# Retention with two tokens to a partition and 64x64 products throughout

## The chip, the cores and the metric

The kernel runs on one core of a Trainium2 chip. TensorE (PE) multiplies; VectorE (DVE) and ScalarE (ACT) do elementwise work and read what TensorE left in PSUM; GpSimd (POOL) here mainly issues DMAs that load and change type; SyncE (SP) issues stores and DMA transposes. Each engine works through its own list in order and waits at semaphores. The metric is the device time in microseconds of one launch. Three runs of the kernel before gave a median of 290.66 us (290.3 to 291.85).

## The reference

Retention over 8 batches, 8 heads, 576 tokens and 64 features a head, then a two-layer product with a hard-swish between:

```python
scores = scale * np.matmul(q, k.transpose(0, 1, 3, 2))          # scale = 1/8
gamma = 1.0 - 2.0 ** (-5.0 - np.arange(H, dtype=np.float32))
Dmat = np.where(rel >= 0, gamma[:, None, None] ** rel[None, :, :], 0.0)   # rel = query - key
ret = np.matmul(scores * Dmat[None, :, :, :], v)
x = ret.transpose(0, 2, 1, 3).reshape(B * S, H * D)             # 4608 x 512
h = x @ w_in                                                    # 512 x 2048
out = (h * np.clip(h + 3.0, 0.0, 6.0) / 6.0) @ w_out            # 2048 x 512
```

## The kernel before

Retention is computed in chunks. A piece is 128 tokens of one batch, with all 8 heads; a batch has four of them, and its last 64 tokens share a piece with those of the next batch ("rest" pieces). There are 36 pieces, and four make a block of 512 tokens, so there are nine blocks. For each piece:

- k and q are brought into a form with the features on the partitions. For pieces 0 to 7 TensorE does it: `k_by_pe` (L318) transposes 128x128 blocks against an identity, `q_by_pe` (L331) multiplies by scaled diagonals in 64x64 products, and ScalarE copies the results out of PSUM. From piece 8 on, SP issues DMA transposes: `transpose_k` (L340) and `transpose_q` (L346), the latter after VectorE has scaled q and v together by powers of gamma (L345).
- `scores` (L356) multiplies k by q for each head, contracting over 64 features; the result is masked by VectorE (L365, L637), half of it by way of a ScalarE copy (`raw`; L767, L633) and a second mask operation (L770).
- `inter` (L282) multiplies q by the running state of the batch, and `intra` (L290) multiplies v by the masked scores; both accumulate in PSUM. The casts at L265 turn them into `xt`, the input of the first matrix product.
- `update_mm` (L384) multiplies k by v, contracting over 128 tokens, and `update_state` (L398 to L402) adds this to the state and decays it.

The first matrix product (`g1`, L411, and L434 for parts of its columns) makes 16 chunks of 128 x 512, each passed through ScalarE (L418) and VectorE (L419). The second is done plainly for block 0 (`g2`, L461), and for blocks 1 to 8 with seven products on half-sized operands (`product`, L520; the sums on VectorE at L494, the results gathered at L530 to L544).

The order of work is written out by hand; there is no planner. The start handles pieces 0 to 3, with filler products on zeros (`warm`, L215) where TensorE would wait. During block 0's second product, steps are put in behind its 16 units, for pieces 4 to 7. `seven_block(kb, mine, next_)` then runs for kb = 1 to 7: between the seven products of block kb it takes the scores of block kb+1's second pair, masks them, does all output products of block kb+1 (`all_outputs`), its state updates and the scores of the first pair of the block after that; then follows the first product of block kb+1. `last_block` does the seven products of block 8, whose rows are the rest tokens, and stores each result as it comes (`store_rest`, L451), on SP and, for the last ones, on ACT's queue too. `store2` (L592) stores the other blocks, `store` (L444) block 0.

Four PSUM banks carry the tag `ph` and are shared by everything; `sc` has two banks, `tu` and `o` one each.

Of the kernel before, what the change touches and what calls it, by code (L numbers as in the profile page):

```python
# [13 lines left out]
ALU = mybir.AluOpType  # L14
# [3 lines left out]
def kernel(  # L18
# [74 lines left out]
    EARLY = 4  # L93
    BY_PE = 8
    SEVEN = 1
    NBUF = 6
    KBUF = 8

    def by_twos(b, s0):

        return q[b, :, s0:s0 + P, :].rearrange("h (g t) d -> g h (t d)", t=2)

    def q2_tile(c):

        tag, bufs = (("part1", 1), ("part5", 1), ("part6", 1), ("osb2", 3))[c % EARLY]
        return work.tile([HALF, H, 2 * D], FP16, tag=tag, bufs=bufs, name=f"q2_{c}")

    def load(c, parts="kqv"):
        if c not in loaded:
            kn = nat.tile([P, H, D], FP16, tag="kn", bufs=KBUF, name=f"kn_{c}")  # L110
            qv = nat.tile([P, 2, H, D], FP16, tag="qv", bufs=NBUF, name=f"qv_{c}")
            loaded[c] = {"kn": kn, "qv": qv}
            if c < BY_PE:
                loaded[c]["q2"] = q2_tile(c)
        to = {"k": (loaded[c]["kn"], k), "q": (loaded[c]["qv"][:, 0], q),
              "v": (loaded[c]["qv"][:, 1], v)}
        for dst, src in (to[part] for part in parts):
            for p0, b, s0, n in pieces[c][3]:
                if src is q and c < BY_PE:
                    nc.gpsimd.dma_start(loaded[c]["q2"], by_twos(b, s0))  # L120
                    continue
                nc.gpsimd.dma_start(dst[p0:p0 + n],  # L122
                                    src[b, :, s0:s0 + n, :].rearrange("h s d -> s h d"))
# [8 lines left out]
    def load_wout(c0, c1):  # L132
# [9 lines left out]
    k0 = work.tile([P, H, D], FP32, tag="osb", bufs=4, name="whole_k_0")  # L142
    nc.sync.dma_start(k0, k[0, :, 0:P, :].rearrange("h s d -> s h d"))
    v0 = work.tile([P, H, D], FP32, tag="osb", bufs=4, name="whole_v_0")
    loaded[0] = {"kn": nat.tile([P, H, D], FP16, tag="kn", bufs=KBUF, name="kn_0"),
                 "q2": q2_tile(0), "v": v0}
    nc.gpsimd.dma_start(loaded[0]["q2"], by_twos(0, 0))
# [11 lines left out]
    two = const.tile([HALF, 2], FP32)  # L159
    e2 = const.tile([HALF, 2, H], FP32)  # L160
    for t in range(2):
        nc.vector.tensor_scalar(out=two[:, t:t + 1], in0=wide[0:HALF, HALF // 2 + 1:HALF // 2 + 2],
                                scalar1=-2.0, scalar2=float(t), op0=ALU.mult, op1=ALU.add)
        nc.vector.tensor_scalar(out=e2[:, t], in0=lnr[0:HALF], scalar1=two[:, t:t + 1],
                                scalar2=None, op0=ALU.mult)
    g2q = const.tile([HALF, 2, H], FP32)
    nc.scalar.activation(g2q, e2, ACTF.Exp)
    tl = const.tile([P, H], FP32)
    nc.vector.tensor_scalar(out=tl, in0=lnr, scalar1=wide[:, HALF + 1:HALF + 2], scalar2=None,
                            op0=ALU.mult)  # L170
    gq = const.tile([P, H], FP32)
    nc.scalar.activation(gq, tl, ACTF.Exp, scale=-1.0)
    gv = const.tile([P, H], FP32)
    nc.scalar.activation(gv, tl, ACTF.Exp, bias=cb[:, 1:2])
    mask_wide = const.tile([P, P + 1], FP16)
    nc.vector.tensor_scalar(out=mask_wide, in0=wide, scalar1=0.0, scalar2=None, op0=ALU.is_ge)
    mask01 = mask_wide[:, 1:P + 1]
    ident16 = const.tile([P, P], FP16)
    nc.vector.tensor_tensor(out=ident16, in0=mask01, in1=mask_wide[:, 0:P], op=ALU.subtract)

    nc.vector.memset(v0[:, 0, 0:1], 0.0)
    nc.sync.dma_start(v0, v[0, :, 0:P, :].rearrange("h s d -> s h d"))
    d2 = const.tile([HALF, 2 * H, HALF], FP16)
    nc.vector.tensor_tensor(
        out=d2, in0=ident16[0:HALF, None, 0:HALF].to_broadcast([HALF, 2 * H, HALF]),
        in1=g2q.rearrange("g t h -> g (t h)")[:, :, None].to_broadcast([HALF, 2 * H, HALF]),
        op=ALU.mult)
    gqv = const.tile([P, 2, H, D], FP16)
    nc.scalar.copy(gqv[:, 1], gv[:, :, None].to_broadcast([P, H, D]))
    nc.scalar.copy(loaded[0]["kn"], k0)  # L190
# [12 lines left out]
    def fill_gq():  # L203
        nc.scalar.copy(gqv[:, 0], gq[:, :, None].to_broadcast([P, H, D]))
# [15 lines left out]
    mask_rest = const.tile([P, P], FP16)  # L220

    def make_mask_rest():
        nc.vector.tensor_copy(mask_rest, mask01)
        nc.vector.memset(mask_rest[0:HALF, HALF:P], 0.0)

    mask_b = {"main": mask01[:, None, :].to_broadcast([P, H, P]),
              "rest": mask_rest[:, None, :].to_broadcast([P, H, P])}
# [5 lines left out]

    class Output:
        def __init__(self, cs, tags):

            self.cs, self.of = cs, len(tags)
            self.n = NCC // self.of
            self.banks = []
            for i, tag in enumerate(tags):  # L240
# [12 lines left out]
        def begins(self, c, h):  # L253
            return c == self.cs[0] and h % NCC < self.of
# [753 lines left out]
```

## Time and profile before

| What | us |
|---|---|
| median of three runs | 290.66 |
| the profiled execution, whole | 289.8 |
| its span | 288.0 |
| TensorE busy | 281.9 |
| VectorE busy | 236.5 |
| ScalarE busy | 163.0 |
| GpSimd busy | 110.7 |

The profile is of one execution. Busy times are those of one engine, with overlapping instructions counted once; the span is from the first instruction to the last. A row of the chain of work gives the start, the length and the engine, tile and line of a stretch that nothing else overlapped on the way back from the last instruction. A row of the groups gives the count of alike instructions, their busy time and the mean of one in ns, then the idle time in front of them and what ended it. "64*64" in a TensorE row is the part of the array that is used, rows by columns. SPq and ACTq are the times in which those engines issue DMAs.

### The profile page before, as it was taken

To read this page: it belongs to the slowest core of one execution; us is meant where nothing else is said; L and a number is where in the kernel's file an instruction comes from. 1 tells how busy PE (TensorE), PEld (TensorE's weight loads), DVE (VectorE), ACT (ScalarE), POOL (GpSimd) and SP (SyncE) were. 2 spreads that over 40 slices of the span, in tenths; PEclk is the share of its full clock that TensorE was granted. 3 is DMA by queue.
4 is the path that set the end of the run, shared out by engine and by line. 5 is a ranking of instruction groups with operands and counts; after the bars stand their busy time and mean duration, and the time that the engine had idled before them with its cause. 6 is when DMAs were issued, how large, how long until landed. Compare 5 with 4: busy or idle time off the path is not lost.

```text
span 288.0 us, 7104 instructions
## 1 busy us (share of the span) xinstructions
PE 281.9 (98%) x2900; PEld 182.7 (63%) x2900; DVE 236.5 (82%) x403; ACT 163.0 (57%) x267; POOL 110.7 (38%) x146
## 2 busy tenths in 40 slices
PE   8999999999999999999999999999999999999994
PEld 3554446648764786468646874687458745874583
DVE  4687649999989988998799879997999789928951
ACT  5668426784278517861776168715872486337721
POOL 8974569630696107520752064306880000000000
PEclk9999999999999999999999999999999999999998
DMA  9999999999999999991999199948995740021014
GB/s 130 168 189 195 192 167 210 171 132 138 106 183 189 138 85 168 193 118 38 135 198 145 38 144 187 130 57 129 200 121 56 104 127 2 0 76 73 2 36 109
DMA packets 149856, 35.85 MB, mean 124 GB/s; under 512 B 139584, under 2 KB 145728, under 8 KB 149824
## 3 DMA queue, kind: packets, MB, share of 16 engines
q0 software_dynamic: 111712, 18.10, 93.9%
q1 hardware_dynamic: 37808, 17.05, 32.3%
q8 instruction: 22, 0.36, 0.5%
q10 hardware_dynamic: 304, 0.26, 0.3%
q14 instruction: 10, 0.08, 0.1%
HBM read 36.70 MB, written 9.44 MB: 160 GB/s over the span
## 4 chain that ended last, share of the span: by engine, by line
PE 96%; DVE 2%; issue 0%; ACTq 0%; ACT 0%; DVEq 0%
PE ph L411 41%; PE b L520 19%; PE c L520 9%; PE a L520 5%; PE pout L461 5%; PE sc L356 4%; PE o L290 3%; PE warm L215 3%; PE ph L434 2%; PE o L282 1%; PE u L384 1%; DVE at L365 1%; PE trq L331 1%; PE trk L318 1%; ACTq L451 0%
## 5 line engine op out<-in xcount | busy, mean ns | idle before, releaser
L418 ACT ACTIVATE u<-ph,cb 128x512 f32<-128x512 f32 x144 | 98.5, 689 | 25.8 <-PE ph L411 23.3
L419 DVE SCALAR_TENSOR_TENSOR gt<-u,ph 128x512 f16<-128x512 f32 x144 | 95.6, 685 | 18.1 <-ACT u L418 15.9
L411 PE MATMUL ph<-xt,win 128*128 128x512 f16 x488 | 106.6, 379 | 0.0
L411 PEld LDWEIGHTS <-win 128*128 128x128 f16 x552 | 54.0, 98 | 63.2
L122 POOL DMA_DIRECT2D kn<-in_k_dram x39 | 33.4, 863 | 64.3 <-PE u L384 58.7
L520 PEld LDWEIGHTS <-s 128*128 128x128 f16 x512 | 49.8, 98 | 6.2 <-DVE s L494 0.2
L520 PEld LDWEIGHTS <-gt 128*128 128x128 f16 x384 | 35.8, 98 | 7.9 <-DVE gt L419 1.1
L122 POOL DMA_DIRECT2D qv<-in_v_dram x39 | 33.9, 876 | 2.3 <-DMA wout<-in_moe_w_out_dram 1.6
L520 PE MATMUL b<-tw,s 128*128 128x256 f16 x256 | 30.6, 273 | 0.0
L122 POOL DMA_DIRECT2D qv<-in_q_dram x32 | 27.3, 860 | 4.3 <-DMA qv<-in_v_dram 2.1
L265 ACT CAST xt<-o 128x512 f16<-128x512 f32 (+1 forms) x25 | 13.2, 584 | 26.0 <-PE o L290 25.9
L365 DVE TENSOR_TENSOR at<-sc,mask_wide 128x1024 f16<-128x1024 f32 x18 | 22.0, 1220 | 6.5 <-PE sc L356 6.5
L494 DVE TENSOR_TENSOR s<-gt 128x512 f16<-128x512 f16 (+1 forms) x37 | 22.7, 615 | 0.1
L530 ACT COPY part<-b 128x512 f32<-128x512 f32 x14 | 8.2, 586 | 25.6 <-PE b L520 25.6
L755 POOL COPY turn<-vs 128x1 f16<-128x1 f16 x7 | 2.6, 372 | 47.1 <-DVE vs L345 47.1
L345 DVE TENSOR_TENSOR vs<-qv,gqv 128x1024 f16<-128x1024 f16 x28 | 19.2, 686 | 0.4 <-DMA qv<-in_v_dram 0.3
L520 PE MATMUL b<-wout,gt 128*128 128x256 f16 x128 | 15.6, 273 | 0.0
L520 PE MATMUL b<-tw,gt 128*128 128x256 f16 x128 | 15.4, 273 | 0.0
L520 PE MATMUL a<-wout,gt 128*128 128x256 f16 x128 | 15.3, 273 | 0.0
L520 PE MATMUL c<-wout,s 128*128 128x256 f16 x128 | 15.3, 273 | 0.0
L520 PE MATMUL c<-tw,s 128*128 128x256 f16 x128 | 15.3, 273 | 0.0
L767 ACT CAST raw<-sc 128x512 f16<-128x512 f32 x28 | 15.0, 589 | 0.2 <-PE sc L356 0.2
(83 smaller groups left out, 271.1 us busy)
## 6 DMA issues: line engine op xcount, KB each, us to landing
kn<-in_k_dram POOLq DMA_DIRECT2D x31, 128.0 KB, 6.8
qv<-in_v_dram POOLq DMA_DIRECT2D x31, 128.0 KB, 7.6
out_dram<-olo SPq DMA_DIRECT2D x7, 512.0 KB, 3.9
out_dram<-ohi SPq DMA_DIRECT2D x7, 512.0 KB, 5.3
qv<-in_q_dram POOLq DMA_DIRECT2D x24, 128.0 KB, 7.3
wout<-in_moe_w_out_dram POOLq DMA_DIRECT2D x4, 512.0 KB, 12.3
q<-in_q_dram POOLq DMA_DIRECT2D x8, 128.0 KB, 6.1
win<-in_moe_w_in_dram POOLq DMA_DIRECT2D x8, 128.0 KB, 6.1
```

The costliest lines, as they stand in the source:

```text
L122: nc.gpsimd.dma_start(dst[p0:p0 + n], src[b, :, s0:s0 + n, :].rearrange("h s d -> s h d"))
L265: engine(xt_of(kb)[:, i::self.of, g0:g0 + len(self.cs) * P], self.banks[i].rearrange("x a c s -> x a (c s)"))
L345: nc.vector.tensor_tensor(out=vs, in0=loaded[c]["qv"], in1=gqv, op=ALU.mult)
L356: nc.tensor.matmul(banks[h2][t, p, :], qk[r, 1, p, t], qk[r, 0, p, :], start=True, stop=True)
L365: mask = lambda: nc.vector.tensor_tensor(out=at.rearrange("t a b s -> t (a b) s"), in0=sc.rearrange("t a b s -> t (a b) s"), in1=mask_b[pi ...
L411: nc.tensor.matmul(ph, win16[:, dmc, P * fc:P * fc + P], xt_of(kb)[:, dmc, :], start=(dmc == 0), stop=(dmc == NCC - 1))
L418: nc.scalar.activation(u, ph, ACTF.Relu, bias=cb[:, 0:1], scale=1.0 / 6.0)
L419: nc.vector.scalar_tensor_tensor(out=gts[kb][:, fc, :], in0=u, scalar=1.0, in1=ph, op0=ALU.min, op1=ALU.mult)
L461: nc.tensor.matmul(pout, gt[:, fc, P * mc:P * mc + P], wout16[:, fc, :], start=(fc == 0), stop=(fc == NFC - 1))
L494: nc.vector.tensor_tensor(out=sm[i][:, q], in0=one, in1=other, op=op)
L520: nc.tensor.matmul(my[chain][tt], left[:, k, P * tt:P * tt + P], right[:, k, :], start=(first and (tt == 0 or apart) and k == 0), stop=(k ...
L767: nc.scalar.copy(raw[:, h2], banks[h2])
```

## The change

All of q, k and v is loaded in one form. Two neighbouring tokens go to one partition: partition g of a half tile holds tokens 2g and 2g+1 of the piece, 512 bytes in a row for a head, where before a partition held one token and 256 bytes (q of pieces 0 to 7 was already loaded so). Two pieces, a pair, are stacked in one tile, the even piece on partitions 0 to 63 and the odd one on 64 to 127. Inside a piece the order of tokens is therefore even ones first, then odd ones; the outputs are stored with a row step of two, and each store becomes one DMA for each parity (in the last block also one for each batch and half).

All retention products become 64x64 in the array: 64 features or 64 token pairs to contract, 64 to put out, with the two pieces of a pair in the two halves of the rows. Products that were made once over 128 tokens are made twice, once for each parity. Before the second half of the state products stands a drain of TensorE, so that two row halves don't write into one bank together. The decay of the keys moves from v to k: for pieces from 8 on, VectorE scales k and q (`scaled`) and leaves v as it is, and the DMA transposes take 128 x 1024 of a pair at once. For pieces 0 to 7 both k and q are turned by 64x64 products (`turn`), and v is scaled in place. The written order at the start and around block 0 is new, as below; two fillers fewer stand there.

```diff
+    def load(c, parts="kqv"):
+        k2, par = divmod(c, 2)
...
+                r = par * HALF + p0 // 2
+                nc.gpsimd.dma_start(
+                    dst[r:r + n // 2],
+                    src[b, :, s0:s0 + n, :].rearrange("h (g t) d -> g h (t d)", t=2))
...
+    def inter_half(pair, turn):
+        order = [(pair[1 - turn], (0, 4), (2, 6)), (pair[turn], (1, 5), (3, 7))]
+        for i in range(2):
+            for o, *heads in order:
+                for h in heads[i]:
...
+                        nc.tensor.matmul(
+                            o.at(h, g), state[rows(h % 2), h // 2, :],
+                            turned(o.c // 2)[rows(h % 2), 1, h // 2, :, at + g.start:at + g.stop],
...
+    def intra(pair):
+        for cc in range(NCC):
+            for t in range(2):
+                for o in pair:
+                    k2, par = divmod(o.c, 2)
+                    for half in range(2):
+                        h = half * NCC + cc
+                        nc.tensor.matmul(
+                            o.at(h), loaded[k2]["v"][rows(par), h, t * D:t * D + D],
+                            st[k2]["at"][rows(par), h % 2, h // 2, t],
...
+    def transpose(k2, which):
+        scaled(k2, which)
+        nc.sync.dma_start_transpose(
+            turned(k2)[:, which].rearrange("x p t s -> x (p t) s"),
+            st[k2]["ks"][:, which].rearrange("s p t a d -> s (p t a d)"))
+    def begin(k2, tags=("ph", "ph")):
...
+        for p in range(NPAIR):
+            for t in range(2):
                 for h2 in range(2):
+                    for par in range(2):
+                        to = sc[:, h2] if p < 2 else more[h2]
...
+        for h2 in range(2):
+            nc.scalar.copy(raw[:, h2], more[h2])
...
+        def mask(i):
+            for h2 in range(2):
+                nc.vector.tensor_tensor(
+                    out=at[:, h2, 2 * i:2 * i + 2].rearrange("x p t u g -> x p (t u g)"),
+                    in0=(raw if i else sc)[:, h2].rearrange("x p t s -> x p (t s)"),
...
     def store_rest(mc, n, cols, src, queues):
-        rows = out.rearrange("(b s) n -> b s n", s=S)
-        for i, queue in enumerate(queues):
-            at = rows[2 * mc + i:2 * (mc + n - 1) + i + 1:2, MAIN:S, cols]
-            queue.dma_start(at.rearrange("t r n -> r t n"), src[i * HALF:i * HALF + HALF])
+        by_b = out.rearrange("(b s) n -> b s n", s=S)
+        quarter = HALF // 2
+        for j in range(n):
+            for t, queue in enumerate(queues):
+                for i in range(2):
+                    r = t * HALF + i * quarter
+                    queue.dma_start(by_b[2 * (mc + j) + i, MAIN + t:S:2, cols],
+                                    src[r:r + quarter, j])
...
+    turn(2, Q)
+    warm(2, MBLK)
+    output_new(0, ("tu", "o"))
+    turn(3, K)
+    warm(2, MBLK)
+    turn(3, Q)
+    warm(2, MBLK)
+    mask = begin(1)
+    mask(0)
     scale_v(1)
+    mask(1)
...
+    def outputs_two(pair, u_tags, between):
...
+        inter_half(pair, 0)
+        for p, t in steps:
+            u_mm(cs[0], p, t, True)
...
+        nc.tensor.drain()
...
+        inter_half(pair, 1)
+        intra(pair)
+        between()
+        for o in pair:
+            o.cast(nc.scalar.copy)
+    def step_four():
+        def between():
+            waiting["mask"] = begin(3)
+        outputs_two([Output(4, "ph"), Output(5, "o")], ("tu",), between)
+        waiting["mask"](0)
+        scale_v(3)
+        waiting["mask"](1)
         update_state(4)
         update_state(5)
     def step_six():
+        outputs_two([Output(6, "sc"), Output(7, "ph")], ("tu", "o"), lambda: None)
...
+    def all_outputs(mine, next_, ready):
+        pairs = [[Output(mine[0], "sc"), Output(mine[1], "ph")],
+                 [Output(mine[2], "ph"), Output(mine[3], "ph")]]
+        if not is_new(mine[0]):
+            for pair in pairs:
+                inter_half(pair, 0)
+            nc.tensor.drain()
+            for pair in pairs:
+                inter_half(pair, 1)
         engines = [nc.vector.tensor_copy] + [nc.scalar.copy] * 3
+        for pair in pairs:
+            intra(pair)
+            for o in pair:
+                o.cast(engines.pop(0))
+        update_mm(list(mine))
         if next_:
+            ready(next_[0] // 2)
+            load_until(next_[1] + GROUP)
...
+    steps = {3: [(turn_two, 4, "tu", "o")], 6: [(make_mask_rest,)], 9: [(turn_sc, 5)],
+             10: [(begin_by_pe, 2, ("tu", "o")), (turn, 6, K)], 11: [(turn, 6, Q, "tu")],
+             12: [(turn_two, 7, "o", "ph")], 13: [(step_four,)],
+             14: [(transpose, 4, K)]}
```

## The prediction

> **What bounds the kernel now.** I read the page's engine line first, then the chain of work that ended last, then the timelines of the places where the chain leaves TensorE.
>
> ```profile
> PE 281.9 (98%) x2900; PEld 182.7 (63%) x2900; DVE 236.5 (82%) x403; ACT 163.0 (57%) x267; POOL 110.7 (38%) x146
> PE 96%; DVE 2%; issue 0%; ACTq 0%; ACT 0%; DVEq 0%
> q0 software_dynamic: 111712, 18.10, 93.9%
> ```
>
> TensorE is busy nearly all the time and carries 96% of the chain. The load queue is as full (93.9%), but no DMA stands on the chain: loads are hidden. So half as many packets is worth nothing by itself, and the change can gain only by shortening TensorE's row of work, and lose wherever TensorE comes to wait. One steady stage of the chain in order of time (start, us, what), and the rest block's form of the same:
>
> ```profile
> 105.35 1.75 PE c L520 x16
> 107.10 0.57 PE o L282 x32
> 107.67 1.01 PE o L290 x32
> 108.68 0.50 PE u L384 x32
> 109.19 0.60 PE sc L356 x16
> 109.78 1.85 PE b L520 x16
> 254.24 0.64 PE o L282 x64
> ```
>
> A full-array group costs 1.75 behind its like and 1.85 behind retention; the seam is a price of about 0.1. State products (L282) are 64x64 already: 32 of 128 columns in 0.57, 17.8 ns each. In the rest block 64 of 64 columns took 0.64, 10 ns each.
>
> The chain leaves TensorE at the start, where masks bind, in the first block of seven products, and at the end:
>
> ```profile
> 14.10 1.23 DVE at L365
> 15.71 0.41 PE o L290 x8
> 16.12 0.98 PE ph L434 x8
> 18.99 12.09 PE ph L411 x56
> 54.74 10.36 PE ph L411 x48
> 76.30 1.14 DVE at L365
> ```
>
> **The change part by part.** Prices of VectorE and ScalarE operations, by groups:
>
> ```profile
> L637 DVE TENSOR_TENSOR at<-sc,mask_wide 128x512 f16<-128x512 f32 x2 | 1.4, 684 | 0.0
> L637 DVE TENSOR_TENSOR at<-raw,mask_wide 128x512 f16<-128x512 f16 x2 | 0.8, 420 | 0.0
> L345 DVE TENSOR_TENSOR vs<-qv,gqv 128x1024 f16<-128x1024 f16 x28 | 19.2, 686 | 0.4 <-DMA qv<-in_v_dram 0.3
> L305 DVE TENSOR_TENSOR vs<-qv,gqv 128x512 f16<-128x512 f16 x6 | 2.5, 411 | 0.0
> L365 DVE TENSOR_TENSOR at<-sc,mask_wide 128x1024 f16<-128x1024 f32 x18 | 22.0, 1220 | 6.5 <-PE sc L356 6.5
> L770 DVE TENSOR_TENSOR at<-raw,mask_wide 128x1024 f16<-128x1024 f16 x12 | 8.3, 692 | 0.0
> L767 ACT CAST raw<-sc 128x512 f16<-128x512 f32 x28 | 15.0, 589 | 0.2 <-PE sc L356 0.2
> ```
>
> *Loads.* Same count and bytes, half the descriptors, one more on POOL's queue (v of piece 0). Worth nothing: no wait on the chain ends on them.
>
> Prices on TensorE at the start: fillers, a transpose of k, and what a turn will be like.
>
> ```profile
> 1.19 3.59 PE warm L215 x8
> 6.86 0.75 PE warm L215 x3
> 34.53 0.22 PE trk L318 x4
> 34.76 0.37 PE trq L331 x16
> ```
>
> *Start-up, +1.2.* Pieces now go in pairs. A pair's masks and v scaling are 2x0.684 + 2x0.411 + 2x0.420 = 3.03 us on VectorE, about 2.75 with the overlap that neighbours show, and its output products need all of it. From 4.79, where the eight fillers end, four turns at 0.37 and nine fillers at about 0.27 (0.25 once the clock is up) put the first pair's scores at 9.0 to 9.45. Masks end at 12.05; two turns and five fillers (2.0) cover to 11.45, so 0.6 of idle. Output products, two turns behind ScalarE's cast and two copies (0.59 each), and the second pair's scores end at 15.2. Its masks run to 17.8, while TensorE has only 0.98 of columns (L434): 1.6 idle. Then 0.45 of outputs, 0.52 of state updates (64 at 8 ns) and 0.98 bring the L411 stream to 19.8 to 20.6, against 18.99: I take +1.2. Ends: -0.5 (first loads land sooner and move it all up) and +3 (a whole mask chain of 3.03 uncovered).
>
> *Block 0's second product, 31 to 55 us, +2.4.* Work: four k transposes become turns, 4x(0.37-0.22) = 0.6. State updates of 64 rows use one row half at a time, 4x0.25 against 0.61: +0.4. Two drains at 0.2: +0.4. Fewer shape seams: -0.3. That is +1.1. Waits: the scores of pair 2 stand one 0.87 unit behind a turn whose two copies take 1.18: 0.3. In the fourth step, pair 3's two raw copies are issued ahead of the two output casts: 4x0.59 = 2.36 after the scores, while TensorE has two units, 1.73, before it needs the casts: 0.65. In the sixth step the update bank is freed by VectorE after 2.75 of masks and three state operations of 0.42, 4.0, while TensorE arrives after 1.73+0.65+0.98+0.22 = 3.6: 0.4. Together 1.35. Ends: +0.5 (covers hold) and +4.5 (waits and drains double).
>
> *First block of seven, +0.8.* The mask row at 76.30 binds already. Per pair the masks go from 1.22+0.69 to 2.2 (+0.3), the scaling from 2x0.686 to 4x0.411 (+0.27), and two masks and one scaling lie ahead: +0.87. Ends 0 and 1.6.
>
> For the output stages: a state product's own length, VectorE's idle, and a transpose with the scores that need it.
>
> ```profile
> L282 PE MATMUL o<-qk,ts 64*64 64x128 f16 x192 | 4.1, 218 | 0.2 <-DVE at L365 0.2
> 113.26 0.69 DVE L419 SCALAR_TENSOR_TENSOR gt<-u,ph 128x512 f16<-128x512 f32 x1 [0.86 <-ACT u L418]
> 136.68 0.69 DVE L540 TENSOR_TENSOR olo<-part,c 128x512 f32<-128x512 f32 x1 [0.72 <-PE c L520]
> 133.65 1.19 SPq L346 DMA_TRANSPOSE qk<-vs x1
> 138.16 0.59 PE sc L356 x16
> ```
>
> *Seven output stages, +0.2 in all.* Without seams 32 products of 128 columns at four at once are 0.45, so state products 0.57 (one seam), output products (64) 0.89, updates 64 at 8 ns in 0.52, scores 32 in 0.45: 2.43 against 0.57+1.01+0.50+0.60 = 2.68, which is -0.25. The drain between the halves of the state products has no row here; the nearest is the seam, 0.1, and the farthest the 0.22 that one such product lasts (218 ns), so I take 0.2, with 0 and 0.5 as ends. The last two outputs are now cast only after all of their pair's products, so the second half of the next scores may wait 0.1 for a bank. So +0.05 each, -0.12 in the block without state products. Ends -1.8 and +3.5 over all.
>
> VectorE's extra 1.1 a block is hidden here: 0.3 in the 0.86 of idle at 113, 0.57 in the 0.72 at 136. With that cover gone it would cost its full 0.3 to 0.6. The q transpose of the next first pair, one DMA of 1024 columns for two of 512, is issued at about 133.9; at twice 1.19 of issue plus about 0.8 it lands by 137.1 to 137.9, before the scores at 138.16. That cover is thin.
>
> *The end, +3.3.* One store of the last block becomes four (32 rows, one token parity, one batch each): 8, 8 and 4 on SP for three 128-row results and 4 on ACT, then 2+2 for each of the two last pieces.
>
> ```profile
> L451 SPq DMA_DIRECT2D out_dram<-endc x5: 490/595/600, 281.2 to 284.7; - x5
> L451 ACTq DMA_DIRECT2D out_dram<-endc x3: 496/515/745, 282.6 to 284.7; - x3
> L444 SPq DMA_DIRECT2D out_dram<-osb x4: 332/348/360, 42.8 to 50.8; - x4
> L586 ACT COPY endc<-b 128x256 f32<-128x256 f32 x2 | 0.7, 373 | 4.9 <-PE b L520 4.9
> 281.16 4.05 SPq L451 DMA_DIRECT2D out_dram<-endc  x5
> 282.57 0.74 ACTq L451 DMA_DIRECT2D out_dram<-endc  x1
> 284.72 0.50 ACTq L451 DMA_DIRECT2D out_dram<-endc  x1
> ```
>
> From 281.16 SP has 16 issues in line; none is hidden, since TensorE is finishing. A smaller store has no row: between 0.348 and 0.595 each, and I take 0.45, below the 64-row stores. The last then starts at 281.16 + 15x0.45 = 287.9 against 284.7: +3.2. On ACT, four issues stand ahead of the copy of the next to last result, two ahead of the last one: 282.57 + 4x0.5 + 0.4 + 2x0.5 + 0.4 + 0.5 = 286.9, +2.2, so SP sets the end. Ends: 15x0.348 gives +1.7, 15x0.595 gives +5.4. Stores of the main blocks also double (issue 0.35 to 0.6 more); SP has room there.
>
> The sum: 1.2+2.4+0.8+0.2+3.3 = +7.9. The profiled execution took 289.8 (span 288.0), 0.9 below the median of 290.66: 297.7.
>
> **The rivals.** *Faster, by the seams.* The change removes some 25 places where the shape of products changes (13 in the output stages, a dozen in blocks 0 and 1), more than the text above credits with 0.1 to 0.15. If each were worth the whole 0.5, 12 us would go, outweighing 7.9, and the kernel takes 285.7; at the 0.15 of the rows 25 places are 3.8, half of it already in the sum. It decides from about 0.4 a seam. For: seams are visible. Against: 1.85 less 1.75 is 0.1. The Trainium skill, "TensorEngine Tiling (Array Packing)", Key Properties, says that changing the tiling mode drains the engine, which speaks for this rival; the trace agrees in kind, with 0.10 in a place, and so the size, not the rule, keeps the chance low.
>
> *About equal.* Issue prices under 0.2 at the end and mask chains covered at the start leave 1 to 2 us: 291.
>
> *Slower still, by transposes or VectorE.* Issue to landing of the q transposes of 512 columns:
>
> ```profile
> DMA to landing us min/median/max: 2.4/4.2/9.3
> ```
>
> My allowance for 1024 columns, 3.2 to 4.0, is below this median for 512. If they land 2 us after 137.5, behind loads and stores, TensorE waits 1.3 in six blocks: 305.5. The same follows if scaling in runs of 64 elements goes at the 0.684 of f32: 8x0.27 = 2.2 a block more, past VectorE's idle. For: landings reached 9.3. Against: half the load packets, and no wait of this kind on the chain now.
>
> *Slower, by issue.* The four groups of an output stage and its other scores grow from 128 products to 224 plus 32. Were 25 ns the least between products, 256 would take 6.4 a stage against 3.2, some 20 us in all: 318. The row at 254.24, 10 ns, excludes it. The Trainium skill, "TensorE: Matmul & The Clock Gate", on the 56 ns gap, gives such a floor of about 25 ns; the trace disagrees for quarter-array products, so it gets 0.02.
>
> **How the numbers follow.** My forecast 0.62 (own range 293.5 to 302), later transposes or VectorE 0.16, issue 0.02, faster 0.11, equal 0.09. The range goes from the equal case, 291.5, to the late transposes, 304.5; it leaves out faster, issue and the ends. 0.5% of 290.66, 1.45, is about what a measurement here can tell from no change: faster 0.11, same 0.09, slower 0.80.
>
> **What would show it.** At the start: L411's counterpart begins at 19.8 to 20.6, idle before the second output products ended by VectorE. Steady: a period near 29.5 without idle on TensorE. At the end: SP in issue without pause after the last results, 16 in line. Wrong would make it: a period under 29.2 (seams), idle before the first scores of a stage ended by a DMA (transposes), or SP issues under 0.3 each.

## The result, and the profile after

| | us |
|---|---|
| before, median of 4 runs beside the kernel after | 291.25 (290.3 to 294.3) |
| after, median of 4 runs | 316.4 (314.01 to 318.56) |
| ratio after to before, 95% interval | 1.084 (1.072 to 1.096) |
| predicted | 297.7 (291.5 to 304.5) |
| the profiled execution after, and its span | 318.56, 316.8 |

Slower, as predicted, but by 25 us where 7 were forecast, and outside the range. The runs of the kernel after lie 4.5 us apart, so a single run of a variant is not read by its time below, but by the stretches of its trace. The page of the kernel after, to be held against the first fence of the prediction:

```profile
PE 293.6 (93%) x3762; PEld 187.8 (59%) x3762; DVE 240.1 (76%) x471; ACT 165.8 (52%) x271; POOL 91.6 (29%) x147
PEclk9995999999995999999999999999999999999998
...
q0 software_dynamic: 62064, 18.23, 54.8%
...
q8 instruction: 29, 0.48, 0.6%
...
PE 84%; issue 4%; DMA 4%; POOL 2%; DVE 2%; ACT 1%; ACTq 0%; POOLq 0%; DVEq 0%
```

TensorE is busy 11.7 us longer (stretches at half clock included), and its idle time grew from 6 to 23. The time that the load packets took fell as planned (54.8% against 93.9%), which no wait needed. New are 4% of "issue" on the chain, that is, mostly TensorE standing still without a wait that the profile shows, and two slices at about half the granted clock. The 4% of DMA and 2% of POOL are mostly the first 19.5 us, which the chain follows back through a load of `w_in` that lands at 19.51, as the second mask operation begins. That operation follows the first by 0.61 in warm11 too (told of below), where no load stands there, and the first one waits for the scores: the load is taken for a coincidence. TensorE's waits of the kernel after (us in total, times, longest) say the same; the kernel before has no line "issue" in this view:

```profile
PE u L381 <- issue: 5.4, 3, 2.0
PE sc L349 <- issue: 4.6, 3, 3.7
PE turn L316 <- ACT kq L168: 1.0, 1, 1.0
PE ph L443 <- ACT xt L247: 0.9, 2, 0.6
PE turn L316 <- ACT qk L319: 0.7, 1, 0.7
PE u L381 <- DVE ta L410: 0.3, 1, 0.3
```

The chain of the kernel after in order of time (start, us, what): the start, the first stage of outputs, two later ones with such a pause, and one without:

```profile
21.25 0.31 PE o L281 x8
...
22.62 2.01 issue
...
24.90 1.82 PE ph L443 x8
26.72 13.97 PE ph L420 x56
...
93.25 0.30 PE sc L349 x7
93.55 3.67 issue
...
98.17 3.53 PE b L534 x16
...
129.21 1.89 issue
...
190.89 1.53 issue
...
220.11 0.35 PE o L267 x16
220.46 0.10 issue
220.55 0.42 PE o L267 x16
220.97 0.89 PE o L281 x64
221.86 0.57 PE u L381 x64
222.44 0.59 PE sc L349 x32
```

The stream of block 0 begins at 26.72 (18.99 before). At 93.55 TensorE stops in the middle of the scores for 3.67, and the 16 products behind take 3.53 instead of 1.85: half clock (the granted clock is 0.50 from 95.25 to 102.08). The stage at 220.11 shows what a stage costs without a pause.

The span cut at the starts of the eight-chain streams (L411 before, L420 after), with the last experiment, best3, told of below, beside it:

| stretch | before | after | difference | best3 less before |
|---|---|---|---|---|
| start to block 0's stream | 18.99 | 26.72 | +7.7 | +5.0 |
| block 0's stream | 12.09 | 13.97 | +1.9 | 0.0 |
| block 0's second product, to 54.74 / 68.11 | 23.66 | 27.42 | +3.8 | +3.8 |
| to the next stream (first block of seven) | 27.36 | 33.58 | +6.2 | +2.4 |
| the next six | 175.64 | 181.83 | +6.2 | +3.4 |
| the last stream to the end | 30.26 | 33.28 | +3.0 | +0.6 |
| span | 288.0 | 316.8 | +28.8 | +15.1 |

The span grew by 28.8 where the medians differ by 25.2, since the profiled execution is the longest of the four.

### The profile page after: what moved, and what is told of

Same layout as the page of the kernel before. It is cut to its first block, busy times and chain, and to the rows that moved or that the text cites. A ratio compares the mean times of both kernels' runs of the same rounds, so it can differ in the third digit from the quotient of the medians.

```text
span 316.8 us, 8889 instructions
## 1 busy us (share of the span) xinstructions
PE 293.6 (93%) x3762; PEld 187.8 (59%) x3762; DVE 240.1 (76%) x471; ACT 165.8 (52%) x271; POOL 91.6 (29%) x147
## 3 DMA queue, kind: packets, MB, share of 16 engines
q0 software_dynamic: 62064, 18.23, 54.8%
## 4 chain that ended last, share of the span: by engine, by line
PE 84%; issue 4%; DMA 4%; POOL 2%; DVE 2%; ACT 1%; ACTq 0%; POOLq 0%; DVEq 0%
PE ph L420 38%; PE b L534 18%; PE c L534 8%; PE a L534 5%; PE pout L475 4%; PE sc L349 3%; PE o L281 3%; PE u L381 2%; PE o L267 2%; DMA v<-in_v_dram 2%; DMA win<-in_moe_w_in_dram 2%; POOL kq L108 2%; PE ph L443 1%; DVE at L362 1%; PE turn L316 1%
## 5 line engine op out<-in xcount | busy, mean ns | idle before, releaser
L420 PE MATMUL ph<-xt,win 128*128 128x512 f16 x488 | 108.9, 384 | 0.0
L420 PEld LDWEIGHTS <-win 128*128 128x128 f16 x552 | 54.6, 99 | 65.1 <-issue 2.5
L534 PEld LDWEIGHTS <-s 128*128 128x128 f16 x512 | 49.9, 98 | 6.1 <-DVE s L508 0.2
L108 POOL DMA_DIRECT2D v<-in_v_dram x40 | 27.7, 696 | 62.2 <-PE u L381 59.0
L534 PEld LDWEIGHTS <-gt 128*128 128x128 f16 x384 | 36.6, 100 | 8.5 <-DVE gt L428 1.1
L362 DVE TENSOR_TENSOR at<-sc,mask_main 128x512 f16<-128x512 f32 x32 | 20.5, 682 | 21.7 <-PE sc L349 21.7
L108 POOL DMA_DIRECT2D kq<-in_k_dram x39 | 26.4, 679 | 15.5 <-PE o L267 10.3
L534 PE MATMUL b<-tw,s 128*128 128x256 f16 x256 | 30.6, 273 | 0.0
L108 POOL DMA_DIRECT2D kq<-in_q_dram x40 | 27.5, 688 | 4.9 <-DMA wout<-in_moe_w_out_dram 2.5
L247 ACT CAST xt<-o 128x512 f16<-128x512 f32 x24 | 12.7, 594 | 30.1 <-PE o L281 30.1
L357 ACT CAST raw<-sc 128x512 f16<-128x512 f32 x36 | 19.3, 589 | 13.6 <-PE sc L349 13.6
L329 DVE TENSOR_TENSOR ks<-kq,gqk 128x512 f16<-128x512 f16 x56 | 21.1, 418 | 0.0
L349 PE MATMUL sc<-qk 64*64 64x128 f16 x576 | 13.4, 228 | 4.6 <-issue 4.6
L534 PE MATMUL b<-tw,gt 128*128 128x256 f16 x128 | 17.0, 291 | 0.0
L534 PE MATMUL b<-wout,gt 128*128 128x256 f16 x128 | 15.6, 273 | 0.0
L319 ACT CAST qk<-turn 128x512 f16<-128x512 f32 x16 | 9.1, 592 | 12.2 <-PE turn L316 12.1
L534 PE MATMUL a<-wout,gt 128*128 128x256 f16 x128 | 15.3, 273 | 0.0
```

Of the source, the lines that this page charges most:

```text
L108: nc.gpsimd.dma_start(dst[r:r + n // 2], src[b, :, s0:s0 + n, :].rearrange("h (g t) d -> g h (t d)", t=2))
L247: engine(xt_of(kb)[:, :, g0:g0 + P], self.bank.rearrange("x a t g -> x a (t g)"))
L329: nc.vector.tensor_tensor(out=ks[:, which, :, t], in0=x[:, :, :, t], in1=gqk[:, which, :, t], op=ALU.mult)
L349: nc.tensor.matmul(to[rows(par), p % 2, t].rearrange("x (u g) -> x u g", u=2), qk[rows(h2), 0, p, t, rows(par)], qk[rows(h2), 1, p, :, row ...
L357: nc.scalar.copy(raw[:, h2], more[h2])
L362: nc.vector.tensor_tensor(out=at[:, h2, 2 * i:2 * i + 2].rearrange("x p t u g -> x p (t u g)"), in0=(raw if i else sc)[:, h2].rearrange("x ...
```

## What the pauses have in common

I numbered TensorE's records in the trace (weight loads, products, waits) in order. The kernel before has 5828, the kernel after 7558. Every pause of TensorE for "issue" above 0.5 us in the kernel after ends at a record whose number leaves 193 when divided by 256, and ends 1.39 to 1.46 us after a 16 KB packet of the instruction queue (q8: 29 packets, 0.48 MB) has landed:

| record | record 256 earlier (us) | packet | pause | TensorE goes on |
|---|---|---|---|---|
| 705 | 18.50 | 22.30 to 23.20 | 2.0 | 24.63 |
| 2497 | 91.53 | 94.92 to 95.82 | 3.7 | 97.22 |
| 3265 | 127.49 | 128.45 to 129.70 | 1.9 | 131.10 |
| 4033 | 158.73 | 158.87 to 159.82 | 0.7 | 161.21 |
| 4801 | 189.14 | 189.99 to 190.96 | 1.5 | 192.42 |
| 5569 | 220.06 | 218.55 to 219.75 | none | 221.99 |

This gave theory A: TensorE runs out of instructions. A stage of outputs and scores is 192 products with a weight load each, 384 records in 2.92 us (at 220.11), where the kernel before has 112 products, 224 records, in 2.68. By this theory a stage pauses or not by where its edges of 256 fall, and by when the fetch begins. Theory B, the rival: the layout itself is dear (drains, seams, quarter-array products), and the pauses belong to it wherever the edges fall. Theory C, for the start: the clock stays at half after the fillers.

## The experiments

**pad15 and pad98: the edges moved.** Small products of zeros in block 1's first product, ahead of the stages, 15 or 98 (30 or 196 records):

```diff
+    def pad(n):
...
+        z = psum.tile([P, 2, NCC * P], FP32, tag="sc", name=f"pad_{padded[0]}")
...
+        for i in range(n):
+            nc.tensor.matmul(z[rows(i % 2), 0, 0:HALF], zeros[0:HALF, 0:HALF],
+                             zeros[0:HALF, 0:HALF], start=True, stop=True)
-    gemm1(1, {1: [(transpose, 5, K)], 5: [(transpose, 5, Q)]}, ())
+    gemm1(1, {3: [(pad, 15)], 1: [(transpose, 5, K)], 5: [(transpose, 5, Q)]}, ())
```

> The changed kernel with 15 small products on zeros (64x64, 64 columns) put into block 1's first product, a seventh unit or so before the first output stage. They cost about 0.2 us and two seams and move every later TensorE instruction back by 30 places in its list. Theory A (TensorE's instructions run out: they come in blocks of 256, and the four long idle times of the changed kernel's output stages all stand at places 193 modulo 256 of the list): the idle times stay at 193 modulo 256. In the stages of blocks 3, 4 and 5 (idle 2.1, 0.9 and 1.7 before) the edges of the instruction blocks move to the stage's beginning and these idle times fall under 0.5; the one of block 2 (3.7) gets shorter or stays; the stage of block 7, without such idle so far, may get 1 to 2. Sum -2 to -5 us. Theory B (TensorE waits for data, for banks or for the drain): the same idle times stand at the same products in the same stages within 0.3, sum +0.5.

> The same with 98 small products, 196 places, some 1.5 us of work. Theory A: the edges of the instruction blocks now fall 35 to 140 places after the beginning of the output stages of blocks 2 to 7, so that most of the 256 instructions between two edges belong to the dense part; each of these stages idles 1.5 to 3 us at a place 193 modulo 256, also those of blocks 6 and 7, which did not. Sum +3 to +8 us against the changed kernel, of which 1.5 is the added work. Theory B: +1.5 and the same idle times at the same products.

Both took the edges with them. With pad15 the pauses of the three blocks at 129, 160 and 191 are gone but for 0.30; the first, at record 2497, stays (4.13 against 3.67). Time 312.15. The chain of pad15:

```profile
91.62 4.13 issue
...
126.88 0.30 issue
```

With pad98 six of the seven stages pause, two that did not before among them (the rows leave out 1.45 at 190.79 and 1.68 at 221.86, of which the chain puts all but 0.38 down to VectorE); time 323.75. The chain of pad98:

```profile
92.93 4.23 issue
97.16 2.72 PE b L544 x12
...
129.15 1.42 issue
...
160.33 1.12 issue
161.45 1.69 PE b L544 x14
...
253.24 2.27 issue
```

At 92.93 and 160.33 the pause stands inside a group of full-array products (L534 in the kernel after). So it does not belong to quarter-array products; it falls where the 256th instruction falls. In both kernels all these pauses, the one at 221.86 too, still end at 193 modulo 256.

**dense_before: more products in the old layout.** In the kernel before, output, update and score products of the blocks from the eighth piece on are cut into two column halves:

```diff
-            nc.tensor.matmul(o.at(c, h), vs[:, h, :], at[:, h % 2, h // 2, :],
...
+            for half in range(2 if c >= BY_PE else 1):
+                cols = slice(half * HALF, half * HALF + HALF) if c >= BY_PE else slice(0, P)
+                nc.tensor.matmul(o.at(c, h, cols), vs[:, h, :], at[:, h % 2, h // 2, cols],
...
```

The updates (2 x 32 columns) and the scores (2 x 64) are cut alike.

> The kernel before the change, with its scores, output and update products of pieces 8 on made in two halves of their columns: same array time and the same results, loads, masks, transposes and order, but 224 more pairs of weight load and product in an output stage and its other scores together, about as many as in the changed kernel. Theory A: idle of 1 to 3 us on TensorE that nothing else ends, at places 193 modulo 256 of its list, in those output stages in which such an edge falls behind the first third; total +5 to +15 us, one or two drops of the granted clock possible. Theory B (the changed layout, drains or loads make the idle): no such idle; total +1 to +3 us from the work of the added instructions alone.

The pauses that theory A expected did not come: 295.55, and the only one is 0.47 at 52.90, in block 0. The halves are slower than I took them to be: 64 update products of 32 columns take 1.00 where 32 of 64 columns took 0.50, so a product of half the columns takes as long. Two rows of its chain:

```profile
109.87 1.14 PE o L292 x64
111.01 1.00 PE u L390 x64
```

With the groups around them that is 192 products in 3.28 us, against 192 in 2.92 in the kernel after: 117 records a microsecond against 132. That is hardly too few, since the bursts of burst_before, below, pause at about 115. What differs is when the fetch began. The edges here lie at 107.94 and 111.16, the first of them still among full-array products, and the packet that was needed at the second had begun at 106.16. In each of the seven stages the packet for the last edge inside began 1.2 to 1.8 us before the edge ahead of it was passed; at the five pauses of the kernel after, where that edge lay among small products, it began 0.1 to 3.8 after. So theory A as the expectation had it, by the place of the edge inside the stage alone, failed; with the begin of the fetch it fits, but that was read afterwards. The 0.6 a stage is the price of the longer row, and makes up most of the time that was added.

**warm11: the clock at the start.** Eleven instead of eight warming products.

```diff
-    warm(8, MBLK)
+    warm(11, MBLK)
```

> The changed kernel with 11 instead of 8 fillers at the very start, so that TensorE is not idle in front of the first turn (0.97 us idle at 4.79 there) and the granted clock need not stay at half until 13.3. Theory C (the late clock is the largest part of the late start): full clock from 6.4 to 10 us on, and the second output products, which waited for masks at 21.25, come 2.5 to 4 us sooner; the first product's stream starts at 22 to 24 instead of 26.7; total -3 to -5 us. Rival (the loads or the mask chain set the start, whatever the clock): less than 1 us sooner.

The chain of warm11:

```profile
6.39 0.54 PE warm L212 x2
...
18.10 0.31 PE o L281 x8
...
19.44 0.40 issue
...
21.08 12.09 PE ph L420 x56
```

The second outputs begin at 18.10 instead of 21.25 and the stream at 21.08 instead of 26.72, at full clock; the expectation had the stream at 22 to 24. In the kernel after TensorE stood idle for 0.97 at 4.79, waiting for ScalarE's cast of the first k (L168): that load lands at 4.66 (3.68 in the kernel before), and the cast, 64x1024 instead of 128x512, takes 1.05 (0.62 before). Behind it two fillers took 1.03 to 1.04 in the timeline until about 12, where here they take 0.60 to 0.61 (0.54 in the chain). So 5.6 of the 7.7 at the start, and the 1.9 in block 0's stream, were the clock and a longer pause (2.01 against 0.40 here; the six added records move that edge too); 2.1 are the new start itself. The pauses in the later stages stay (3.8 us the longest). Time 313.39.

**spread: the same instructions, further apart.** The products of the fifth and seventh chain are put between the groups of small ones; nothing is added or left out. `open_outputs` makes the outputs from the states, `close_outputs` those from the values.

```diff
             both(7)
             gather(kb, 7)
+            pairs = open_outputs(mine)
             both(3)
             gather(kb, 3)
-        all_outputs(mine, next_, ready)
+            close_outputs(pairs)
+            both(4)
+        update_mm(list(mine))
+        if next_:
+            ready(n_one)
...
-        both(4)
         gather(kb, 4)
```

> The kernel after with the same instructions, only ordered apart: in the blocks of seven products the 32 big products of the seventh stand between the outputs and the state updates (in the first such block 16 before and 16 behind the values), and from the second block on the 32 of the fifth chain between the outputs from the states and those from the values. Theory A (the order of instructions runs dry: 448 of them in 2.6 us, while a 16 KB fetch and what follows it takes 1.5 to 5 us): the idle stretches of 3.7, 1.9, 0.7 and 1.5 us in these stages go or fall below 0.5 each, and with the first of them the 6.8 us of half clock behind it; span 316.8 falls by 7 to 11 us. Theory B (the quarter-array products, their drains and seams are dear in themselves, wherever they stand): the stretches stay or move with the products, span within 2 us of the kernel after. The waits at the start (2.0 at 22.6 us) stay under both.

The pauses of the stages at 129, 160 and 191 are gone; in the first one 1.89 of 3.67 is left, with the half clock behind it, and the one at the start stays (1.42). The span fell by 4.7, less than expected, for a reason I had not put in: the masks of the next pair now have no cover, VectorE falls behind, and from the first product of the stream at 127.12 to its end are 14.7 instead of 13.8. The chain of spread:

```profile
92.64 1.89 issue
...
95.75 15.07 PE ph L420 x64
...
128.40 1.63 DVE at L362 x4
130.19 1.27 DVE gt L428 x2
```

**burst_before: many instructions in the old layout.** The kernel before, with 320 products of zeros (64x64 by 64 columns, added work) in the first chain of seven blocks: in one go in blocks 2, 4, 6 and 8, in eight lots of 40 in blocks 3, 5 and 7.

```diff
+        if kb > SEVEN:
+            for j in [7] if kb % 2 == 0 else range(4, 12):
+                steps.setdefault(j, []).append((pad, 320 if kb % 2 == 0 else 40))
```

> The kernel before with 320 products of zeros (64x64 by 64x64, results never read, added work only) in the first chain of each of six blocks: in blocks 2, 4 and 6 all 320 in one go, in blocks 3, 5 and 7 in eight lots of 40 between the large products. At 9 ns each (the state updates of the kernel after: 64 in 0.57 us) they take 2.9 us in a block. Theory A (instruction supply): a burst is 640 instructions and runs dry at its second edge of 256, and at a third where there is one: 1 to 4 us of idle in each of blocks 2, 4 and 6, none above 0.3 in blocks 3, 5 and 7; the burst blocks are longer than the others by 1 to 5 us each. Theory B (the layout of the kernel after, not the number of instructions, makes the idle stretches): both kinds of block are longer by the same 2.5 to 3.5 us, no idle above 0.5.

A product cost 18.7 ns, not 9, so a block got 6.0 longer by the products alone, and with the pauses and half clock behind them the kernel takes 370.09. The chain shows the pauses; first a burst (block 4), then spread ones (block 5), then the last burst (block 8):

```profile
178.17 3.19 PE pad L417 x194
181.36 2.88 issue
...
188.78 2.48 issue
...
220.86 0.75 PE pad L417 x40
221.61 0.97 PE ph L422 x4
...
339.87 0.85 issue
```

The four bursts pause 3.16+4.22, 2.88+2.48 (the second just behind the burst), 2.18 and 0.85 us, all at 193 modulo 256. Of the spread blocks one pauses 1.67, the others at most 0.46. The kernel before, whose trace has no such pause, pauses as soon as it has such a burst (256 records in 2.2 us at 179.14), and hardly where the same number is spread. That is theory A; the 1.67 is a miss of its "none above 0.3" and says that even 256 records in 5 us can be too many: there the fetch began 3.5 us after the edge before, took 1.5, and TensorE went on 1.9 later.

**tail2: the line of stores.**

```diff
-        for j in range(n):
-            for t, queue in enumerate(queues):
-                for i in range(2):
...
+        for t, queue in enumerate(queues):
+            for i in range(2):
+                r = t * HALF + i * quarter
+                at = by_b[2 * mc + i:2 * (mc + n - 1) + i + 1:2, MAIN + t:S:2, cols]
+                queue.dma_start(at.rearrange("j g n -> g j n"), src[r:r + quarter, 0:n])
```

> The kernel after with the last block's stores joined over the two column blocks of a tile: 10 issues on SyncE's and ScalarE's queues behind the last products instead of 20 (the sum of the lines of issues of 0.45 to 0.46 us each falls by 4 to 5 us). If the line of issues at 0.45 each sets the end: the stretch from the last product to the end (306.1+0.9 to 316.8) is shorter by 1.5 to 3 us, all else as in the kernel after. If the landing of the transfers sets it: by less than 0.7 us.

SyncE's issues in the timeline of the kernel after:

```profile
306.94 7.34 SPq L464 DMA_DIRECT2D out_dram<-endc  x16
```

and in that of tail2:

```profile
304.16 4.80 SPq L464 DMA_DIRECT2D out_dram<-endc  x10
```

From the first of these issues to the end of the span are 9.9 in the kernel after and 7.3 in tail2 (6.8 in the kernel before): 2.5 less for six issues less. The line of issues sets the end. (Counted from the first issue, since the chain leaves TensorE at different products in the two kernels.)

**best2: four edits at once.** warm11, tail2, spread with the second half of the last chain left behind the scores, and 30 added products of 4 columns that move the edges to the beginning of the dense stages.

```diff
+            close_outputs(pairs)
+            product(kb, 4, 0)
         update_mm(list(mine))
...
+        if kb > SEVEN:
+            product(kb, 4, 1)
```

> The kernel after with four edits at once: three more warming products at the start; the last stores joined over two column blocks; the products of the seventh and the fifth chain put between the groups of quarter-array products as in the kernel spread, but with the last 16 of the seventh left behind the next scores, so that the masks keep that cover; and 30 products of 4 columns in block 1's first product (60 instructions, added work), which move the edges of 256 instructions from inside the first dense stage to its beginning. Theory A (instruction supply, cold clock and the line of store issues make up what the prediction missed): the parts add: 5 us from the clock at the start, 3 at the end, 9 or more from the idle stretches, so 297 to 304 us, at or just above what was predicted for the change (297.7), and no idle for instructions above 1 us behind 30 us. Theory B (the dense stages are dear in themselves): above 306 us. Under neither is it below the kernel before: the two-token turns and scores of block 0, the drains and the longer first stage stay.

306.31 (306.06 to 307.65), ratio to before 1.053 (1.049 to 1.058). By its time this is theory B's answer, by 0.3; by its trace the seven stages have no pause above 0.3, and two other places have: 2.06 at 19.29 and 1.96 at 54.81, the second a place that had none, behind 30 us, against what theory A said. So the run did not settle how much of the remainder is supply.

**best3: those two pauses taken away by place alone.** The edit is shown against best2; besides, in the first block of seven all 16 last products of the seventh stand behind the scores again.

```diff
-    warm(11, MBLK)
+    warm(5, MBLK)
+    few = psum.tile([P, MBLK], FP32, tag="ph", bufs=4, name="few")
+    for i in range(106):
+        nc.tensor.matmul(few[i % 2 * HALF:i % 2 * HALF + HALF, 0:HALF], zeros[0:HALF, 0:HALF],
+                         zeros[0:HALF, 0:HALF], start=True, stop=True)
...
-    gemm1(1, {3: [(pad, 30)], 1: [(transpose, 5, K)], 5: [(transpose, 5, Q)]}, ())
+    gemm1(1, {3: [(pad, 58)], 1: [(transpose, 5, K)], 5: [(transpose, 5, Q)]}, ())
```

> The kernel best2 with its two idle stretches left for instructions (2.1 us at 19.3, 2.0 at 54.8) tried by their place alone: six of the eleven warming products give way to 106 small ones (64x64 by 64 columns on zeros, added work in the time in which TensorE waits for the first k), so 200 more instructions stand ahead and the edges of 256 fall outside both places; 28 more four-column products in block 1's first product (0.5 us) keep the later edges where they were; in the first block of seven all 16 last products of the seventh stand behind the scores again, so that the masks keep their cover (0.7 us). Theory A (what remains above the prediction is idle for instructions and the half clock behind it): both stretches fall below 0.7, and the time from 306.3 to between 299 and 302.5. Theory B (the remainder is the price of the new layout itself): the stretches move or the time is made up elsewhere, 305 to 307. If small products do not raise the clock, the first turns run at half speed and 2 to 3 us come on top of either.

305.34 (302.86 to 305.62), ratio 1.044 (1.038 to 1.050). Both pauses are gone: TensorE's waits of best3 have no line "issue" left. But the first turns run at half speed, as the last sentence of the expectation feared: two fillers between them take 1.03 to 1.04, and the stream starts at 24.00 instead of 21.08. (The page shows full clock in all 40 slices. The trace has no record of the clock before 13.2 us, and the page counts that as full, so the start is read from the fillers.) The timeline of best3:

```profile
3.44 3.03 PE L218 MATMUL few<-zeros 64*64 64x64 f16 x106
...
6.83 1.04 PE L212 MATMUL warm<-zeros 128*128 128x512 f16 x2
```

With that price, theory A's figure is 301 to 305.5 and theory B's 307 to 310: the run stands at A's upper end. How much of the remainder is supply is thus not settled by this run; that the pauses come with the edges is shown by pad15, pad98 and burst_before. No version of the new layout came near the kernel before.

Of the 15.1 that best3's span still lies above the old one, 2.9 are that cold clock, 1.0 the padding (58 products, 1.01 in the chain), 0.9 a wait that its own order brings (the scores at 91.64 for VectorE's update of a state, which the kernel after has not), and about 1.7 the seams of spreading (six stages: 3.4 over the kernel before, against 0.25 to 0.35 each in the stages of the kernel after that have no pause). That leaves about 8.6, to which the old line of stores adds 2.5: some 11 us for the change without pauses and at full clock. Reckoned from the other side, in the kernel after: 28.8, less 9.8 of pauses, less about 8 of half clock (3.2 before the second outputs, 0.9 in L443, 1.9 in block 0's stream, 1.9 behind the pause at 93.55), is 11. This is an estimate; no run was at full clock throughout and without both the pauses and the added work.

## Why the prediction was right or wrong

**Right: the direction, the end, and what does not matter.** The end was predicted at +3.3 and came to +3.0; the estimate of 0.45 for a store of 32 rows stands against 7.34/16 = 0.46, and SyncE's line sets the end, as tail2 shows. Half the descriptors were worth nothing: in neither kernel does a wait of TensorE's products end on a load, and the one load that bears on the start, the first k, lands 1.0 us later. The 1024-column transposes of q were not late, and VectorE did not overrun in the kernel after: that rival did not happen. It showed that its cover was real only when spread took the cover away. The rival "faster, by the seams" fell: the outputs from the values went from 1.01 to 0.89 a stage, as reckoned, but no stretch got shorter.

**Wrong: the start, +1.2 predicted, +7.7 measured.** The step that failed is "four turns at 0.37 and nine fillers at about 0.27 (0.25 once the clock is up)" from 4.79 on. The sum lets the first turn follow the eight fillers at 4.79, and names "first loads land sooner" as its lower end. The first k landed 1.0 later and its cast took 0.43 longer, so the turn began at 5.76, and the fillers behind it ran at half speed until about 12 (1.03 for two); I had carried the clock over from the kernel before without looking at what fills the gap. With the gap filled the start costs +2.1, within the ends I gave (-0.5 to +3).

**Wrong: "Slower, by issue", 0.02.** The step that failed is "the row at 254.24, 10 ns, excludes it". The count was near (128 products with the other scores become 224; the 32 added there were in them already), the resource was the wrong one. I asked for the least time of a product, and shut the case. That row is short, 64 products, and says nothing of 384 records in one stage. A cost of supplying instructions was put at nothing in the term of +0.2 for seven stages. The limit was the supply: 256 records at a time, whose fetch began 0.1 to 3.8 us after the edge at these five pauses; TensorE went on 1.4 after it had landed. It cost 9.8 us directly and, by the half clock behind two of the pauses, some 4.7 more (0.9 + 1.9 + 1.9). The Trainium skill, "Runtime: NRT & Kernel Launch", Instruction fetch mechanics, describes refills of 16 KiB or 256 instructions, which the trace bears out to the number, and says that the cost of crossing is mostly hidden; that held for the kernel before, and fails here by 0.7 to 3.7 us at five edges. I had this page and no row that would have made me count instructions per microsecond.

**Mis-sized: block 0, +2.4 predicted, +3.8 measured.** TensorE's work rose from 23.66 to 25.31, +1.65 against my +1.1, and the waits came to 2.1 against 1.35. Of those foreseen, the casts behind the raw copies came as 0.9 in two waits (0.65 foreseen) and the update bank as 0.3 (0.4). The 0.3 foreseen for the scores of pair 2 is not among TensorE's waits. Not foreseen was 0.7 of a turn behind ScalarE's copy of the turn before it (L319).

**Mis-sized: the output stages, +0.05 each predicted, +0.25 to +0.35 measured where there is no pause.** The stage at 220.11 adds up to 2.92 against my 2.73. The products from the states took 0.35 and 0.42 with 0.10 of drain between, 0.87 where I had 0.57 and 0.2; the scores 0.59 where I had 0.45. The outputs from the values came at 0.89, exactly as reckoned.

**The first block of seven**, predicted +0.8, came to +6.2, of which 3.67 are the pause and 1.9 the half clock behind it; +0.6 is left.

Without pauses and half clock, by the estimate of 11 above, the sum of 7.9 would have been short by about 3 us: a miss in size, inside the range. With them it is another case, which had no place among my rivals.

## What to carry to other kernels

Count an engine's instructions per microsecond, not only their lengths: where a change halves the size of products and doubles their number, look for stretches in which several hundred run in 2 or 3 us, and put large products between them, or keep the edges of 256 out of them. A pause of two or three microseconds is paid twice, since the clock may fall behind it; and a filler ahead of a late first load has to reach to that load, with large products. Where work is moved to space instructions out, ask what it had been covering.

## What the hardware showed that I had not expected

- *When a fetch begins goes with the other transfers, and with what stands at the edge.* From the passing of an edge to the packet's begin: 3.39 us while 124 GB/s were moved, 0.96 in a stretch without other traffic. The windows of the kernel after (us of the window, then busy time of PE, PEld, DVE, ACT, POOL with counts, clock, DMA share, GB/s):

```profile
91.53:94.92 3.39, 2.02 (x143) 1.73 (x132) 2.63 (x6) 1.56 (x3) 3.31 (x5) 1.00 1.38 124
127.49:128.45 0.96, 0.96 (x75) 0.96 (x78) 0.35 (x2) 0.10 (x1) 0.00 (x0) 1.00 0.00 0
158.73:158.87 0.14, 0.14 (x13) 0.14 (x16) 0.07 (x1) 0.00 (x0) 0.00 (x0) 1.00 0.43 117
...
23.57:30.40 6.83, 5.77 (x22) 2.67 (x23) 3.48 (x7) 2.29 (x4) 2.45 (x4) 0.50 1.34 199
```

  In burst_before the same burst waited 3.0 and 4.8 in block 2 at 241 and 153 GB/s, and 0.7 in block 8 at 25. The row of 0.14 at 117 GB/s does not fit, and where the edge falls among full-array products the packet can begin before it is passed (1.5 us before 220.06). This is an association over a dozen edges; no run changed the traffic alone.
- *The clock halved in a pause of 2.01 us*, for 6.83 us (last row above). The clock fell at 23.57, when TensorE had stood still for 0.95, with waits of 0.52 and 0.43 in the three microseconds before the pause; in the pause of 3.67 at 93.55 it fell after 1.70. A pause of 1.89 at 129.21 in the same kernel left it full. The Trainium skill, "TensorE: Matmul & The Clock Gate", Why this matters for your kernels, puts the bound at about 3 us of idle; in these two pauses the clock fell sooner, after 0.95 and 1.70.
- *Small products did not raise the clock.* 106 of 64x64 in 3.03 us without a gap left it at half in best3, where six full-array products in the same place had it up by 6.4 in warm11. This is one run and one place.
- *Fewer columns do not make a product shorter below some 16 to 19 ns* unless its neighbours use other quarters of the array: 64 updates of 32 columns 15.6 ns each (dense_before), 64-column products that alternate between two halves of the columns 18.7 ns (burst_before), 4-column ones 0.56 us for 30, the same 18.7 (best2); the updates of the kernel after, over all four quarters, 8.9.
